# Pooled attention into a routed MoE: x scatters no longer ordered behind x loads of other slots, and loads issued one by one among the scatters

## The chip, the cores and the metric

The kernel runs on one NeuronCore of one Trainium2 chip. The metric is the device time of one execution in microseconds (us); lower is better. Several executions of each kernel are timed in rounds, beside executions of the kernel before on the same chip. One execution of each kernel is also recorded by the hardware profiler. The **span** is the time from the first to the last instruction in that record.

The engines are PE (matmul), DVE (vector), ACT (scalar), POOL (GpSimd) and SP (sync). In this kernel POOL issues nearly all transfers: the loads of q, k, v and of the weights, and every indirect scatter. SP issues the transposing loads of x. All of them run on the core's 16 DMA engines. In the records, q0 is the queue of POOL's transfers (weights and scatters) and q1 the queue of SP's transposes.

A few of the experiments had executions that took 20 to 40 us longer than others of the same kernel. They are called slow, and no conclusion is drawn from a time that only they show.

## The reference, cut to what matters

```python
# attention: B=8, H=8, S=576, D=64; k and v averaged over 8 tokens -> 72 keys
k_p = k.reshape(B, H, 72, 8, D).mean(axis=3)
v_p = v.reshape(B, H, 72, 8, D).mean(axis=3)
attn = softmax(q @ k_p.T / sqrt(D))
x = (attn @ v_p).transpose(0, 2, 1, 3).reshape(4608, 512)
# MoE: each of 4608 tokens has one of 8 experts (domain_id)
for e in range(8):                       # w1[e] 512x1024, w2[e] 1024x512
    out[domain_id == e] = relu(x[domain_id == e] @ w1[e]) @ w2[e]
```

## The kernel before

The kernel has two stages. The attention stage works on four pairs of batches. It writes each chunk of 128 tokens with an indirect scatter into `x_slots` in DRAM, where every expert has 640 slots; slots that no token fills are cleared by other scatters. In the expert stage each expert's x comes back by a transposing load, is multiplied by w1 and w2, and leaves as five blocks of 128 rows, scattered to `out`. Expert 0 is loaded in two parts. Its first 384 slots hold tokens of the first three pairs and can be loaded early. The other 256 slots, called the **late x of expert 0** below, need the last scatters of the attention stage.

```python
def load_pair(t_ap, pr, tag):                     # L84: one of q, k, v of one pair
    t = wp.tile([128, 72, D], F16, tag=tag, bufs=2, name=tag)
    nc.gpsimd.dma_start(...)                      # on POOL
...
def clear(bl):                                    # L370: zeros into empty slots
    i = nc.gpsimd.indirect_dma_start(
        out=x_slots[:], out_offset=bass.IndirectOffsetOnAxis(ap=void[:, bl:bl + 1], axis=0),
        in_=zt[:], ...)                           # L372
    apart(i.ins, "xs", "no token has an empty slot")
    x_scatters.append(i.ins)
...
            if qd == 1:                           # in av_unit: a chunk of 128 tokens is done
                i = nc.gpsimd.indirect_dma_start(
                    out=x_slots[:], out_offset=bass.IndirectOffsetOnAxis(ap=slot_i[:, c:c + 1], axis=0),
                    in_=x_sb[:], ...)             # L508
                apart(i.ins, "xs", "each token has its own slot")
                x_scatters.append(i.ins)
...
def wload(e, which):                              # L532: 1024 KB as float16, from float32
    ...
    nc.gpsimd.dma_start(t, src)                   # L538, on POOL

def xload(e, s0, s1, pool, tag, after=()):        # L543
    xT = pool.tile([128, 4, s1 - s0], F16, tag=tag, bufs=3 if tag == "xT" else 1, name="xT")
    i = nc.sync.dma_start_transpose(xT[:, :, 0:s1 - s0], x_slots[CAP * e + s0:CAP * e + s1, :])   # L545
    behind(i.ins, x_scatters, "x of the slots")   # after all scatters so far
    ...
def l2_units(e, s0, s1, hT):                      # per block of 128 tokens
    ...
    y = late.tile([128, HD], F32, tag="y", bufs=8, name="y")
    ...                                           # PSUM -> y on DVE or ACT
    i = nc.gpsimd.indirect_dma_start(out=out, ..., in_=y[:], ...)    # L590, on POOL
...
tasks = [(0, 0, EARLY), (0, EARLY, CAP)] + [(e, 0, CAP) for e in range(1, E)]

def fetch(e):
    if e >= 2:
        run(clear_units(e))                       # two scatters
    if e == 1:
        xload(0, EARLY, CAP, late, "xTl")         # the late x of expert 0
    wload(e, 0)
    wload(e, 1)
    xload(e, 0, CAP, late, "xT")

fetch(1)
for n, t in enumerate(tasks):
    ...
    u = expert_units(*t)
    nxt = n + 2
    if nxt < E:
        u = u[:3] + [lambda: fetch(nxt)] + u[3:]  # fetch two tasks ahead
    run(u)
```

The dependency tracker sees that a scatter writes `x_slots` and that a transpose reads it. It does not know which rows an indirect scatter touches. So every scatter waits for every transpose that was issued before it, even for a transpose of other experts' slots.

The softmax here doesn't subtract the row's maximum and nothing guards it: scores larger than these inputs give would overflow.

## Time and profile before

| | before |
|---|---|
| timed, median of 2 (range) | 331.55 us (330.36 to 332.73) |
| profiled execution, its time and span | 317.65 and 315.9 us |
| PE busy | 236.0 us, 75% of the span |
| last part of x made by attention (start of the last x_sb, which takes 0.42 us) | 104.9 us |
| PE idle on the two largest releasers in the expert stage | 28.9 + 25.0 us |

Three lines of the page follow: PE's busy time with its share and number of instructions, and the granted PE clock and the DMA busy share in 40 slices of the span, in tenths.

```profile
PE 236.0 (75%) x1888; PEld 161.2 (51%) x1888; DVE 115.9 (37%) x324; ACT 94.4 (30%) x153; POOL 111.3 (35%) x130
...
PEclk9995995989985569759999996559959999879999
DMA  6999999994249532995966959968959949922112
```

The waits view says what each engine waited for (us in total, times, longest). The first fence is PE, the second POOL.

```profile
PE big L565 <- ACT hT L569: 28.9, 4, 19.4
PE big L565 <- DMA xT<-x_slots: 25.0, 3, 13.6
```

```profile
POOL x_slots L372 <- DMA xT<-x_slots: 84.9, 6, 15.8
...
POOL x_slots L508 <- DMA xT<-x_slots: 12.2, 1, 12.2
```

POOL stood still for 84.9 us in six waits of a clear for somebody else's transpose. The timeline shows what lay behind such a wait. Columns are start, duration, engine, line, operation, and in brackets the idle time before it and what ended it. First POOL around the end of attention, then PE in the expert stage.

```profile
100.83 1.01 POOL L508 DMA_INDIRECT x_slots<-x_sb,slot_i  x1 [0.63 <-DVE rcp L500]
114.03 1.00 POOL L508 DMA_INDIRECT x_slots<-x_sb,slot_i  x1 [12.19 <-DMA xT<-x_slots]
...
125.30 1.19 POOL L538 DMA_DIRECT2D w<-in_moe_w_dram  x2
142.28 1.04 POOL L372 DMA_INDIRECT x_slots<-zt,void  x1 [15.80 <-DMA xT<-x_slots]
143.62 1.03 POOL L372 DMA_INDIRECT x_slots<-zt,void  x1 [0.30 <-issue]
144.64 0.60 POOL L538 DMA_DIRECT2D k<-in_moe_w_dram  x1
```

```profile
113.27 7.20 PE L565 MATMUL big<-xT,w 128*128 128x384 f16 x32 [9.68 <-DMA xT<-x_slots]
...
139.23 6.09 PE L565 MATMUL big<-xT,w 128*128 128x256 f16 x32 [13.58 <-DMA xT<-x_slots]
...
206.94 9.13 PE L565 MATMUL big<-xT,q 128*128 128x320 f16 x48 [19.36 <-ACT hT L569]
```

The weights of expert 2 (tiles k and v at 144.64) could only be issued once the clears at 142.28 had been let go. When outputs queue in POOL behind such a wait, the eight y buffers fill, ACT and DVE stop, and PE stops behind them; that is the 19.36 us. The line at 139.23 is the late x of expert 0, for which PE waited 13.58 us.

### The profile page before, as it was taken

Reading aid. Unit: us, or ns where it says so; the run is one execution under the profiler, and the core shown is the slowest. Engines: PE = TensorE matmul, PEld = TensorE weight load, DVE = VectorE, ACT = ScalarE, POOL = GpSimd, SP = SyncE. Lnnn points to the kernel's source line nnn. Section 1 sums busy time; section 2 is a strip of 40 time slices with the busy share of each in tenths; the row PEclk is TensorE's granted clock in tenths of the full one; section 3 lists DMA queues with packets and bytes.
Section 4 is the critical chain, followed back from the end, with each engine's and each line's share of the span. In section 5 each row is a group of like instructions: output and inputs, shape, how many; then the busy total and the mean of one; then the engine's idle time right before and its main releaser. Section 6 shows DMA issues by size and latency. Waiting matters only on the chain.

```text
span 315.9 us, 4766 instructions
## 1 busy us (share of the span) xinstructions
PE 236.0 (75%) x1888; PEld 161.2 (51%) x1888; DVE 115.9 (37%) x324; ACT 94.4 (30%) x153; POOL 111.3 (35%) x130
## 2 busy tenths in 40 slices
PE   0975979879999069039999950079789899399992
PEld 0753655555665044026949530056456685274950
DVE  6630699879688313002323100022112230122410
ACT  1061874567897011002313000022021130121220
POOL 7000161724776048007005036027045066303232
PEclk9995995989985569759999996559959999879999
DMA  6999999994249532995966959968959949922112
GB/s 127 210 221 211 218 216 223 225 213 167 80 92 216 124 98 104 185 196 101 178 178 117 220 107 187 181 123 165 259 115 190 269 66 216 292 84 98 50 68 97
DMA packets 30602, 51.25 MB, mean 162 GB/s; under 512 B 23340, under 2 KB 23406, under 8 KB 26992
## 3 DMA queue, kind: packets, MB, share of 16 engines
q0 software_dynamic: 9728, 45.63, 63.9%
q1 hardware_dynamic: 20848, 5.28, 8.8%
q8 instruction: 15, 0.25, 0.3%
q14 instruction: 11, 0.09, 0.1%
HBM read 61.90 MB, written 17.30 MB: 251 GB/s over the span
## 4 chain that ended last, share of the span: by engine, by line
DMA 47%; PE 21%; issue 13%; DVE 8%; POOL 6%; ACT 2%; POOLq 1%; SPq 0%; ACTq 0%; DVEq 0%
DMA xT<-x_slots 22%; DMA out_dram<-y,orig 9%; DMA k<-in_k_dram 7%; PE big L565 7%; DMA v<-in_moe_w_dram 4%; PE big L474 4%; DMA x_slots<-x_sb,slot_i 3%; POOL out_dram L590 3%; PE small L496 3%; PE small L403 3%; PE small L432 2%; DVE x_sb L503 2%; DMA x_slots<-zt,void 2%; DVE op L326 1%; POOL x_slots L372 1%
## 5 line engine op out<-in xcount | busy, mean ns | idle before, releaser
L565 PE MATMUL big<-xT,w 128*128 128x320 f16 (+2 forms) x256 | 43.2, 333 | 29.6 <-DMA xT<-x_slots 23.3
L571 DVE TENSOR_SCALAR hT<-big 128x640 f16<-128x640 f32 (+2 forms) x36 | 27.0, 749 | 77.2 <-PE big L565 77.2
L565 PEld LDWEIGHTS <-w 128*128 128x128 f16 x256 | 36.3, 149 | 36.7 <-issue 17.8
L590 POOL DMA_INDIRECT out_dram<-y,orig x40 | 39.8, 996 | 39.9 <-DVE y L586 12.4
L508 POOL DMA_INDIRECT x_slots<-x_sb,slot_i x36 | 37.3, 1036 | 45.4 <-DVE rcp L500 16.5
L581 PEld LDWEIGHTS <-hT 128*128 128x128 f16 x320 | 31.4, 98 | 35.9
L477 ACT ACTIVATE at<-big 72x576 f16<-72x576 f32 x64 | 40.5, 645 | 23.8 <-PE big L474 22.9
L569 ACT ACTIVATE hT<-big 128x640 f16<-128x640 f32 (+2 forms) x36 | 23.2, 644 | 79.3 <-PE big L565 79.3
L372 POOL DMA_INDIRECT x_slots<-zt,void x16 | 15.8, 988 | 88.0 <-DMA xT<-x_slots 84.9
L586 DVE COPY y<-small 128x512 f32<-128x512 f32 x20 | 13.8, 692 | 85.8 <-DMA out_dram<-y,orig 51.8
L588 ACT ACTIVATE y<-small 128x512 f32<-128x512 f32 x20 | 12.0, 598 | 94.9 <-DMA out_dram<-y,orig 52.9
L581 PE MATMUL small<-w,hT 128*128 128x512 f16 x160 | 35.3, 379 | 0.0
L503 DVE TENSOR_TENSOR x_sb<-small,rcp 128x256 f16<-128x256 f32 x72 | 30.5, 424 | 2.5
L565 PE MATMUL big<-xT,q 128*128 128x320 f16 x64 | 11.5, 349 | 21.1 <-ACT hT L569 19.4
L496 PE MATMUL small<-vp,at 72*128 72x65 f16 (+1 forms) x320 | 23.9, 215 | 0.7 <-DVE x_sb L503 0.3
L474 PE MATMUL big<-qT,kpT 64*72 64x288 f16 x128 | 22.7, 350 | 1.3 <-ACT qT L462 0.9
L565 PEld LDWEIGHTS <-q 128*128 128x128 f16 x64 | 9.2, 150 | 23.6 <-issue 21.7
L496 PEld LDWEIGHTS <-at 72*128 72x128 f16 (+1 forms) x320 | 16.1, 112 | 9.0 <-issue 4.0
L565 PE MATMUL big<-xT,k 128*128 128x320 f16 x128 | 17.8, 299 | 0.0
L565 PEld LDWEIGHTS <-k 128*128 128x128 f16 x128 | 17.4, 144 | 0.5
L581 PE MATMUL small<-v,hT 128*128 128x512 f16 x80 | 17.6, 379 | 0.0
L403 PE MATMUL small<-k,ident 128*128 128x320 f16 (+1 forms) x64 | 13.2, 349 | 3.6 <-DMA k<-in_k_dram 3.6
(137 smaller groups left out, 221.1 us busy)
## 6 DMA issues: line engine op xcount, KB each, us to landing
w<-in_moe_w_dram POOLq DMA_DIRECT2D x8, 1024.0 KB, 9.0
k<-in_k_dram POOLq DMA_DIRECT2D x4, 1152.0 KB, 22.3
q<-in_q_dram POOLq DMA_DIRECT2D x4, 1152.0 KB, 27.9
v<-in_v_dram POOLq DMA_DIRECT2D x4, 1152.0 KB, 19.8
k<-in_moe_w_dram POOLq DMA_DIRECT2D x3, 1024.0 KB
v<-in_moe_w_dram POOLq DMA_DIRECT2D x3, 1024.0 KB, 13.8
q<-in_moe_w_dram POOLq DMA_DIRECT2D x2, 1024.0 KB
out_dram<-y,orig POOLq DMA_INDIRECT x40, 12.0
```

The lines of the kernel that those rows point to most:

```text
L372: i = nc.gpsimd.indirect_dma_start(out=x_slots[:], out_offset=bass.IndirectOffsetOnAxis(ap=void[:, bl:bl + 1], axis=0), in_=zt[:], in_offs ...
L403: nc.tensor.matmul(pv, ident[:], kk[:, t, w0:w1, :], start=(t == 0), stop=(t == 7))
L474: nc.tensor.matmul(p[0:72, par, 0:288], s["kpT"][64 * par:64 * par + 64, bh, :], s["qT"][64 * par:64 * par + 64, :, 8 * bh:8 * bh + 8], st ...
L477: nc.scalar.activation(at[0:72, bh % 8, :].rearrange("p (a c) -> p a c", a=2), p[0:72, :, 0:288], AFT.Exp, scale=1.0 / 64.0)
L496: nc.tensor.matmul(pv[r0:r0 + z - a, hh, :], s["at", bt][0:72, h, a:z], s["vp"][0:72, 8 * bt + h, :], start=True, stop=True, skip_group_ch ...
L503: nc.vector.tensor_tensor(out=xo, in0=pv[:, :, 0:64].rearrange("p h (a b) -> p b h a", b=4), in1=rcp[:].unsqueeze(1).unsqueeze(3).to_broad ...
L508: i = nc.gpsimd.indirect_dma_start(out=x_slots[:], out_offset=bass.IndirectOffsetOnAxis(ap=slot_i[:, c:c + 1], axis=0), in_=x_sb[:], in_of ...
L565: nc.tensor.matmul(p[:, a, 0:m], w1[:, kk, fi:FF:8], xT[:, kk, m * a:m * a + m], start=(kk == 0), stop=(kk == 3))
L569: nc.scalar.activation(dst, p[:, 0:nh, 0:m], AFT.Relu)
L571: nc.vector.tensor_scalar(out=dst, in0=p[:, 0:nh, 0:m], scalar1=0.0, scalar2=None, op0=ALU.max)
L581: nc.tensor.matmul(p[:], hT[:, fi, 128 * j:128 * j + 128], w2[:, fi, :], start=(fi == 0), stop=(fi == 7))
L590: i = nc.gpsimd.indirect_dma_start(out=out, out_offset=bass.IndirectOffsetOnAxis(ap=orig[:, bl:bl + 1], axis=0), in_=y[:], in_offset=None, ...
```

## The change

The intent: take the false order between scatters and transposes away, so that POOL never waits for a transpose, and spread POOL's loads among the scatters of the attention stage so that no scatter stands behind several loads at once and the weights of experts 0 and 1 are there early.

```diff
@@ clear(), and the same in av_unit() for the scatters of tokens
             apart(i.ins, "xs", "no token has an empty slot")
+            tc.declare_no_dep(i.ins, group="xl", reason="the slots read so far are other experts'")
             x_scatters.append(i.ins)
@@ xload()
-        def xload(e, s0, s1, pool, tag, after=()):
+        def xload(e, s0, s1, pool, tag):
...
+            tc.add_to_no_dep_group("xl", i.ins)
             behind(i.ins, x_scatters, "x of the slots")
-            behind(i.ins, after, "one transfer at a time")
@@ where the plan of the attention stage is made
-        put(clear_units(0) + clear_units(1), 33.0, 40.0)
-        put([lambda: loads(2)], 4.9, 5.0)
-        put([lambda: loads(3)], 15.4, 15.5)
-        put([lambda: wload(0, 0)], 43.0, 43.1)
-        put([lambda: wload(0, 1)], 52.1, 52.2)
-        put([lambda: xload(0, 0, EARLY, per, "xTe")], 52.3, 52.4)
+        for pr in range(2, NP):
+            for d, t_ap, tag, kx in ((kt, k, "k", 6.0), (vt, v, "v", 10.0), (qt_, q, "q", 14.0)):
+                put([lambda d=d, t_ap=t_ap, pr=pr, tag=tag: load(d, t_ap, pr, tag)],
+                    16 * pr - 32 + kx, 16 * pr - 32 + kx)
+        put([lambda: wload(0, 0)], 38.0, 38.0)
+        put([lambda: wload(0, 1)], 43.0, 43.0)
+        put(clear_units(0), 44.0, 46.0)
+        put([lambda: xload(0, 0, EARLY, per, "xTe")], 52.3, 52.3)
+        put(clear_units(1), 60.0, 61.0)
+        put([lambda: wload(1, 0), lambda: wload(1, 1)], 62.0, 63.0)
@@ fetch()
             if e >= 2:
                 run(clear_units(e))
-            if e == 1:
+                wload(e, 0)
+                wload(e, 1)
+            else:
                 xload(0, EARLY, CAP, late, "xTl")
-            wload(e, 0)
-            wload(e, 1)
             xload(e, 0, CAP, late, "xT")
```

(The helper `loads(pr)` for three loads becomes `load(...)` for one.) The change has two parts: the **no-dependence part** (three added lines) and the **placement part** (the rest). A transpose still waits for all scatters issued before it.

More of the change, by code (lines that the diff above doesn't have):

```diff
@@ L511, in av_unit @@
                 apart(i.ins, "xs", "each token has its own slot")
+                tc.declare_no_dep(i.ins, group="xl", reason="the slots read so far are filled by other tokens")
                 x_scatters.append(i.ins)
@@ L617, in put, with load @@
                 plan.append((k0 + (k1 - k0) * (i + 0.5) / len(units), len(plan), f))
-        def loads(pr):
-            kt[pr] = load_pair(k, pr, "k")
-            vt[pr] = load_pair(v, pr, "v")
-            qt_[pr] = load_pair(q, pr, "q")
+        def load(d, t_ap, pr, tag):
+            d[pr] = load_pair(t_ap, pr, tag)
         for pr in range(NP):
```

## The prediction

> **What bounds the kernel now.** PE is 75% busy, DMA 73% (queue list). The attention stage (to 103 us) is nearly PE-bound: PE 14 to 18 us busy in each 17 to 19 us window. The loss is in the expert stage. In the chain of waits the x transposes (xT<-x_slots) are the largest entry, 22% of the span. The waits view says why: POOL's clearing scatters (L372) waited 84.9 us in six times for a transpose of *another* expert to land, and a scatter of L508 12.2 us. POOL works in order, so the next weights and the output scatters stood behind these waits. Outputs came late, the eight y buffers filled, and PE waited: 28.9 us put down to ACT hT (really y and PSUM buffers; DVE and ACT waited 51.8 and 52.9 us for out_dram scatters) and 25.0 us for xT: 54 us idle. Expert DMA comes in saturated bursts (146 to 162 us, 168 to 184, 188 to 210) with gaps.
>
> **What the change does.** No arithmetic is added or removed. In the instruction lists clears and scatters lose only the transpose waits; transposes still wait for scatters. The weights of experts 0 and 1 move forward among the scatters, into a stretch where DMA is under half busy (79 to 98 us: 0.45). The pair loads move later: v2, q2, k3, v3, q3 by about 10 to 20 us. They landed 5 to 20 us ahead of need, so I expect no new stall over 3 us.
>
> **Costed.**
> - Attention ends at about 103 us as before.
> - The first x load landed at 113.3; it should land by 103: the first expert part (12.5 us of PE) starts 8 to 10 us sooner.
> - POOL issues one scatter per 1.29 us and is backlogged from 75 us in both kernels. Without the 12.2 us wait the last scatter goes at about 113 (before 124.3). The late x of expert 0 lands at 120 to 125 instead of 139; PE waits 4 to 9 us instead of 13.6.
> - From there PE needs 10 us for the rest of expert 0 and 17.7 us (8.9 + 8.8) for each of seven more: 134 us, to about 257.
> - DMA, estimated from the bursts: two weights and one x about 14 us, one output scatter about 1.25 us; after 117 us some 140 us of work. So they nearly balance, and I allow 6 us for stalls. Tail after PE 6 us as now.
>
> The Trainium skill, "DMA: Bandwidth & Descriptors", section "Issuing engines are not separate DMA queues", says that all issuers' transfers interleave on the same 16 engines. This trace agrees: a transpose lands in 3.9 us alone, 17.2 us (median) beside weights. So overlap is not free.
>
> Span about 269 us (315.9 before); the timed runs lie 15.7 us above the span, so 284 us, 8 in 10 between 271 and 300. Faster by over 2%: 0.96; same 0.03; slower 0.01.
>
> **What would show it.** L372 waits for xT vanish; PE idle on ACT hT falls from 28.9 to under 8 us; idle on xT from 25 to under 12; DMA share after 113 us rises from about 0.68 to over 0.85; attention end stays within 3 us of 103; last L508 scatter near 113.
>
> **What would make it wrong.** DMA limiting the expert stage (transposes beyond 20 us, outputs queued behind weights, y buffers full again): 295 to 305. Late q3 or v3 stalling attention: some us more. A lower granted clock.

## The result, and the profile after

| | before | after |
|---|---|---|
| timed, median (range), 2 executions each | 331.55 us (330.36 to 332.73) | 301.3 us (300.52 to 302.08) |
| ratio after / before | | 0.9088, 95% interval 0.8916 to 0.926 |
| span of the profiled execution | 315.9 us | 300.4 us |
| start of the last x_sb | 104.9 us | 127.0 us |
| PE resumes with the late x of expert 0 | 139.23 us | 163.05 us |

A ratio in this document is the mean time of one kernel's fast runs over the mean of the other's of the same rounds, so it is not quite the ratio of the medians that are quoted. The change is faster by 9.1%, as predicted in direction, but 301.3 us lies 17 us above the predicted 284 and just outside the range that ended at 300.

The same three lines of the page, after:

```profile
PE 236.1 (79%) x1888; PEld 164.7 (55%) x1888; DVE 117.5 (39%) x324; ACT 95.1 (32%) x153; POOL 110.5 (37%) x130
...
PEclk9995898776987955579555799999999999999998
DMA  6999989897975824698999949999999994302112
```

The waits of PE and of POOL, after:

```profile
PE big L567 <- DMA xT<-x_slots: 23.7, 1, 23.7
```

```profile
POOL out_dram L592 <- ACT y L590: 65.3, 18, 27.3
POOL x_slots L509 <- DVE rcp L501: 44.3, 9, 26.7
```

POOL no longer waits for a transpose at all. The waits it has now are for data to be scattered, which is idle time that costs nothing. PE's 28.9 us on hT are gone too. One wait is left, longer than any before: 23.7 us, once, for a transpose. POOL around the end of attention, then PE:

```profile
130.76 0.98 POOL L509 DMA_INDIRECT x_slots<-x_sb,slot_i  x1 [0.30 <-issue]
...
136.13 0.58 POOL L540 DMA_DIRECT2D k<-in_moe_w_dram  x1 [1.81 <-DMA x_slots<-x_sb,slot_i]
136.69 0.59 POOL L540 DMA_DIRECT2D v<-in_moe_w_dram  x1
...
143.88 0.60 POOL L540 DMA_DIRECT2D q<-in_moe_w_dram  x1
144.47 0.58 POOL L540 DMA_DIRECT2D k<-in_moe_w_dram  x1
```

```profile
125.80 8.34 PE L567 MATMUL big<-xT,w 128*128 128x384 f16 x32
...
163.05 6.62 PE L567 MATMUL big<-xT,w 128*128 128x256 f16 x32 [23.74 <-DMA xT<-x_slots]
...
172.97 8.90 PE L567 MATMUL big<-xT,w 128*128 128x320 f16 x64
...
190.34 8.90 PE L567 MATMUL big<-xT,k 128*128 128x320 f16 x64
```

From 163 us on PE works without a pause, one expert in 17.4 us (190.34 less 172.97), to the end. The late x is read by PE 32 us after the last token scatter at 130.76; before, that was 15 us (139.23 less 124.34). In between POOL has issued the weights of experts 2 and 3, four loads, the first at 136.13 us; before, the first of these loads went at 144.64 us, after the transpose had landed. (The tiles named k, v and q hold weights here: k and v at 136 us are those of expert 2, q and k at 144 us those of expert 3.)

The table by stretch says the same. Columns are the stretch, its length, busy time and instructions of each engine, the mean granted clock, the DMA share and GB/s. First before, then after.

```profile
141.00:170.00 29.00, 29.00 (x175) 21.55 (x174) 7.90 (x12) 7.63 (x13) 10.28 (x12) 0.95 0.66 131
170.00:206.00 36.00, 15.88 (x92) 10.75 (x91) 3.85 (x5) 2.45 (x5) 9.30 (x11) 0.80 0.90 179
206.00:236.00 30.00, 25.85 (x127) 16.93 (x127) 6.83 (x9) 6.09 (x10) 11.03 (x13) 0.79 0.75 163
```

```profile
141.00:170.00 29.00, 6.95 (x35) 5.44 (x36) 1.56 (x4) 1.54 (x4) 3.44 (x5) 0.53 1.05 217
170.00:206.00 36.00, 36.00 (x216) 25.79 (x215) 10.20 (x14) 8.62 (x13) 15.95 (x18) 1.00 0.91 176
206.00:236.00 30.00, 30.00 (x187) 23.09 (x186) 8.88 (x12) 8.03 (x12) 13.64 (x16) 1.00 1.12 229
```

In the stretch from 141 to 170 us PE does 6.95 us of work while the DMA engines are full (1.05). Everywhere later PE is full at a clock of 1.00.

### The profile page after: what moved, and what is told of

It reads as the page before. It is cut to its first block, busy times and chain, and to the rows that moved or that the text cites. A ratio compares the mean times of both kernels' runs of the same rounds, so it can differ in the third digit from the quotient of the medians.

```text
span 300.4 us, 4759 instructions
## 1 busy us (share of the span) xinstructions
PE 236.1 (79%) x1888; PEld 164.7 (55%) x1888; DVE 117.5 (39%) x324; ACT 95.1 (32%) x153; POOL 110.5 (37%) x130
## 4 chain that ended last, share of the span: by engine, by line
issue 33%; DMA 22%; PE 19%; POOL 13%; DVE 6%; ACT 2%; another core or an unknown queue 1%; POOLq 1%
POOL out_dram L592 9%; DMA k<-in_k_dram 7%; DMA out_dram<-y,orig 6%; PE big L475 5%; DMA v<-in_moe_w_dram 4%; PE small L497 4%; DMA w<-in_moe_w_dram 4%; PE small L433 3%; PE small L404 3%; DVE x_sb L504 2%; POOL x_slots L372 1%; PE small L446 1%; PE small L461 1%; DVE qT L465 1%
## 5 line engine op out<-in xcount | busy, mean ns | idle before, releaser
L509 POOL DMA_INDIRECT x_slots<-x_sb,slot_i x36 | 36.4, 1012 | 69.4 <-DVE rcp L501 44.3
L567 PE MATMUL big<-xT,w 128*128 128x320 f16 (+2 forms) x256 | 41.7, 329 | 23.8 <-DMA xT<-x_slots 23.7
L478 ACT ACTIVATE at<-big 72x576 f16<-72x576 f32 x64 | 40.8, 645 | 41.3 <-PE big L475 27.1
L497 PE MATMUL small<-vp,at 72*128 72x65 f16 (+1 forms) x320 | 25.3, 220 | 7.4 <-DVE rcp L501 2.5
L475 PE MATMUL big<-qT,kpT 64*72 64x288 f16 x128 | 24.1, 372 | 4.9 <-issue 1.7
L497 PEld LDWEIGHTS <-at 72*128 72x128 f16 (+1 forms) x320 | 17.0, 115 | 16.9 <-issue 6.1
L433 PE MATMUL small<-ident,v 128*128 128x128 f16 x144 | 17.6, 275 | 7.0 <-DVE kpT L397 5.5
L501 DVE RECIPROCAL rcp<-small 128x4 f32<-128x4 f32 x72 | 12.7, 176 | 17.9 <-PE small L497 10.3
L433 PEld LDWEIGHTS <-v 128*128 128x128 f16 x144 | 12.1, 124 | 10.5 <-issue 7.7
L567 PEld LDWEIGHTS <-k 128*128 128x128 f16 x128 | 17.4, 144 | 0.5
L372 POOL DMA_INDIRECT x_slots<-zt,void x16 | 15.7, 983 | 4.9 <-issue 4.9
```

Source lines behind the costliest of these rows:

```text
L372: i = nc.gpsimd.indirect_dma_start(out=x_slots[:], out_offset=bass.IndirectOffsetOnAxis(ap=void[:, bl:bl + 1], axis=0), in_=zt[:], in_offs ...
L433: nc.tensor.matmul(pv[:, i, :], vv[:, o:o + 128], ident[:], start=(t == 0), stop=(t == 3), skip_group_check=True)
L475: nc.tensor.matmul(p[0:72, par, 0:288], s["kpT"][64 * par:64 * par + 64, bh, :], s["qT"][64 * par:64 * par + 64, :, 8 * bh:8 * bh + 8], st ...
L478: nc.scalar.activation(at[0:72, bh % 8, :].rearrange("p (a c) -> p a c", a=2), p[0:72, :, 0:288], AFT.Exp, scale=1.0 / 64.0)
L497: nc.tensor.matmul(pv[r0:r0 + z - a, hh, :], s["at", bt][0:72, h, a:z], s["vp"][0:72, 8 * bt + h, :], start=True, stop=True, skip_group_ch ...
L509: i = nc.gpsimd.indirect_dma_start(out=x_slots[:], out_offset=bass.IndirectOffsetOnAxis(ap=slot_i[:, c:c + 1], axis=0), in_=x_sb[:], in_of ...
```

## The experiments

Two questions were open. First, the absolute level: attention ended near 127 us in the profile after, but at 104.9 us in the profile before. Either the edit delays attention, or the execution profiled before was a faster one than the timed ones (called the level theory: T2 in the first expectations, P in the last). Second, the late x of expert 0, with two theories. **S**, starvation: the transpose's small packets share the DMA engines with the new weights and only get through when the weights are done. **R**: the last scatters end late, and the transpose has to wait for them. All outputs of all runs were correct. Runs on one chip: e1 to e4; e5 to e8; e9 to e11; e12 to e14.

### Both kernels again, and each part alone

e1_before is the kernel before, unchanged; e2_after the changed kernel, unchanged.

> The kernel before, unchanged, profiled on the same chip as the next three. Theory T1 (the moved loads lengthen the attention stage, from 103 to 125 us): attention ends near 103 us here and the span is near 316 us. Rival T2 (the attention stage varies from chip to chip whatever the placement; the timed runs of before were 331 us against a profiled execution of 317.65): attention ends well after 103 us here, 115 us or more, and the span is near 330 us.

> The changed kernel, unchanged, on the same chip. T1: attention ends near 125 us as in the first profile, over 15 us later than in e1_before. T2: it ends within 5 us of where it ends in e1_before. Both: the second x load of expert 0 takes over 20 us to land, and from there to the end about 137 us.

e3_nodep is the kernel before with only the no-dependence part:

```diff
--- before
@@ clear() and av_unit()
+            tc.declare_no_dep(i.ins, group="xl", reason="...")
@@ xload()
+            tc.add_to_no_dep_group("xl", i.ins)
```

> Only the first part of the change: clears and scatters not ordered behind x loads; loads where they were before. T1: attention ends near 103 us as in before, the late x of expert 0 lands 20 us or more after its issue, because weights of experts 1 to 3 are issued beside it; total 300 us or less, better than or equal to the whole change. If T1 is wrong and the placement is what gains: over 315 us.

e4_place is the changed kernel without those three lines, so only the placement part:

```diff
--- after
@@ clear() and av_unit()
-            tc.declare_no_dep(i.ins, group="xl", reason="...")
@@ xload()
-            tc.add_to_no_dep_group("xl", i.ins)
```

> Only the second part: loads one by one among the scatters; clears and scatters still ordered behind x loads. T1: attention ends near 125 us, no gain or slower than before (325 to 340 us), since the waits of POOL for transposes (85 us) are back. T2: attention as in e1_before, total a few us under before.

| run | this, median us | before, median us | ratio (95%) | start of last x_sb | PE resumes with late x |
|---|---|---|---|---|---|
| e1_before | 332.6 | 331.44 | 1.0071 (0.999 to 1.0153) | 124.3 | 152.46 |
| e2_after | 299.61 | 331.44 | 0.9055 (0.8981 to 0.9128) | 124.4 | 161.21 |
| e3_nodep | 303.14 | 331.44 | 0.9144 (0.9051 to 0.9236) | 128.2 | 164.76 |
| e4_place | 323.6 | 331.44 | 0.9782 (0.9696 to 0.9868) | 121.5 | 146.26 |

The level theory holds. The unchanged kernel's attention ends at 124.3 us here, with a span of 328.2, and the changed kernel's at 124.4. The edit does not delay attention. The profile taken before the prediction was of an execution that took 317.65 us, while the timed ones took 330 to 333.

The no-dependence part alone brings 8.6%, the placement part alone 2.2%, both together 9.5% in the same rounds; the parts nearly add (10.8% against 9.5%). POOL's waits view of e4_place shows that placement leaves the false waits as they were:

```profile
POOL x_slots L372 <- DMA xT<-x_slots: 85.2, 6, 16.2
```

In e2_after and e3_nodep there is no such line, and none of PE waiting for hT either; in e4_place PE still waits 24.9 us for hT. So the mechanism that the change aims at is shown: with the false order of the scatters the wait for hT stands, without it the wait is gone.

From PE's resumption with the late x to the end of the span, e1_before takes 328.2 - 152.46 = 175.7 us and e2_after 298.2 - 161.21 = 137.0 us. The expert stage gains 38.7 us there; 8.8 us of it are given back because the late x is read 8.8 us later.

### What holds the late x of expert 0

e5_hold2 lets the first weights of expert 2 wait for the late x; e6_hold3 does so with those of expert 3 only, so that expert 2's still run beside it. POOL issues in order, so everything after is held too.

```diff
--- after
-        def wload(e, which):
+        def wload(e, which, after=()):
...
-            nc.gpsimd.dma_start(t, src)
+            i = nc.gpsimd.dma_start(t, src)
+            behind(i.ins, after, "weights not beside the x load that is waited for")
...
+        urgent = []
@@ fetch()
-                wload(e, 0)
+                wload(e, 0, urgent if e == 2 else ())     # e6_hold3: e == 3
...
-                xload(0, EARLY, CAP, late, "xTl")
+                urgent.extend(xload(0, EARLY, CAP, late, "xTl"))
```

> The changed kernel, with one wait added: expert 2's first weight load (and all that GpSimd issues after it) waits until the second x load of expert 0 has landed. Theory S (starvation: transposes get few packets while weight packets are queued, so that x load lands only when the queue runs dry, at about 160 us in e2_after, although issued at 135 us): it lands within 5 us of its issue, PE idle on it falls from 24.8 to under 4 us, total 275 to 281 us. Rival R (the x load is late because the last scatters land late, behind the weights of expert 1): at most 3 us gained, 296 to 300 us.

> The same wait one expert later: only expert 3's weights are held; expert 2's (2 loads) are issued beside the x load as in the changed kernel. S: the x load lands when the queue runs dry of two loads less, about 10 us earlier than in e2_after; PE idle on it 12 to 17 us; total 286 to 292 us. R: no gain, 296 to 300 us.

e7_w1early instead brings expert 1's weights forward, before the last nine token scatters; e8_both has this and the edit of e5_hold2.

```diff
--- after
-        put([lambda: wload(1, 0), lambda: wload(1, 1)], 62.0, 63.0)
+        put([lambda: wload(1, 0), lambda: wload(1, 1)], 54.0, 56.0)
```

> The changed kernel with expert 1's weights issued before the last nine scatters instead of before the last five, no hold. R: the last scatters land about 5 us earlier and the x load with them: 5 to 10 us gained, 290 to 295 us. S: the amount queued behind is the same, the x load lands when it is drained: 295 to 300 us; the first x load of expert 0 may be delayed by some us as it now meets these weights.

> Hold of e5 and early weights of e7 together. S: as e5, plus up to 5 us from scatters that land earlier, if the first x load is not delayed past the end of attention: 271 to 280 us.

| run | all its times, us | before, median us | ratio of fast runs (95%) |
|---|---|---|---|
| e5_hold2 | 342.58, 328.03, 319.88, 332.4 | 331.19 | none |
| e6_hold3 | 323.37, 293.13, 311.76, 291.94, 290.68 | 331.19 | 0.8825 (0.872 to 0.893) |
| e7_w1early | 371.76, 345.86, 365.76, 377.14 | 331.19 | none |
| e8_both | 323.26, 295.49, 329.64, 297.26, 293.4 | 331.19 | 0.8941 (0.8831 to 0.905) |

The late x itself is decided before the slow stretches of these profiles begin (about 188 us in e5_hold2, 176 us in e6_hold3), so it can be read from them. PE's timeline, one line each of e2_after, e5_hold2 and e6_hold3:

```profile
161.21 6.01 PE L567 MATMUL big<-xT,w 128*128 128x256 f16 x32 [24.82 <-DMA xT<-x_slots]
```

```profile
141.83 4.43 PE L568 MATMUL big<-xT,w 128*128 128x256 f16 x32 [2.15 <-DMA xT<-x_slots]
```

```profile
154.01 5.77 PE L568 MATMUL big<-xT,w 128*128 128x256 f16 x32 [15.12 <-DMA xT<-x_slots]
```

The wait is 24.8 us with four weight loads let loose beside the transpose (e2_after), 15.12 us with two, and 2.15 us with none. SP issued the late x at 135.45, 137.58 and 138.02 us, so it was no earlier where the wait is short. That is a dose and its response, and it refutes R as the whole cause: with the scatters where they were, the wait all but vanishes. Packet counts from the same records show how. This is a count of the packets that started in each 4 us, worked out from the traces: q1 is the transposes (nearly all of 256 bytes), q0 the KB that weights and scatters moved.

```
us from            132    136    140    144    148    152    156    160    164
before      q1     115   2521    994      0     55     95    262   2180      0
            q0 KB  792    272      0    341    824    752    900     52      0
e2_after    q1       0      6    109    128    345    121    230   3315   3075
            q0 KB  806    688    776    700   1097    832    744      0      0
e5_hold2    q1       0    529   2941    192    115    107    364    113     99
            q0 KB  744    486      0    744    792    636   1137    768    808
e6_hold3    q1       0      0     66     96    458   3403    825    124    115
            q0 KB  868    457    784    744    929     52    496    864    744
```

In every row the transposes move over 2,000 packets per 4 us only where q0 is nearly dry, and 55 to 460 where it is full. (In e2_after the first packet of the late x starts at 139.6 us, so its 6 says nothing.) In e2_after from 140 to 158 us, 756 transpose packets (27 ns each) started beside 758 packets of q0: 374 of 8 KB, which are weights and took 657 ns each, 205 of 4 KB, which are scattered outputs, and small ones. The Trainium skill, "DMA: Bandwidth & Descriptors", section "Queues, rings and completion order", says under Arbitration that each DMA engine goes round between the queues it has work for, a packet at a time. The trace agrees, if a packet of its records is one of the page's: 756 to 758 is one for one; it is 761 to 762 in the first profile after (142 to 160 us) 338 to 338 in e6_hold3 (142 to 151 us), and 115 to 115 in the kernel before (132 to 136 us). An estimate from these numbers: the late x has 1,024 packets (the 5,120 slots take 20,480), 64 for each of the 16 engines; at one per 8 KB packet of 657 ns it would take 42 us. The 758 turns were too few for it, so it landed only when q0 had run dry, at 161.17 us. Theory S holds.

The row of the kernel before shows the irony. There the late x landed at 136 to 140 us, because the next weights stood behind a clear that waited for a transpose. Even there it took 12.2 us (SP issued it at 126.98, it landed at 139.18), beside the weights of expert 1 that POOL had issued at 125.30; in e4_place, where those are loaded earlier, it took 3.8 us (142.46 to 146.21). The false wait that the change removes had also kept the weights out of the way of the one load that PE needed next.

Holding back only the weights of expert 2 doesn't settle it. In e5_hold2 the weights of experts 2 and 3 were issued together after the hold, and from 144 us on the next x met both (the row shows 99 to 364 packets beside a full q0); PE waited 18.4 us for it at 185.72 us. The starvation had moved one expert on. The time expected for e5_hold2, 275 to 281 us, was missed by far; its only fast time, 319.88 us, has no profile, so how much of that the slow transposes took is not known. e6_hold3 came near what was expected (286 to 292 us; fast runs 290.68 to 293.13). e8_both, expected at 271 to 280 us, took 293.4 to 297.26 us in its fast runs, though PE did not wait for the late x in its profile.

Three of e7_w1early's four executions are slow, the profiled one of 371.76 us among them. Before its slow stretch, which begins at about 152 us, it shows two things more. The first x load of expert 0 took 10.1 us on SP instead of 1.5, beside expert 1's weights. And PE did not wait for the late x, without any hold:

```profile
142.13 4.38 PE L567 MATMUL big<-xT,w 128*128 128x256 f16 x32
```

SP issued it at 132.83 us, a microsecond before POOL issued the next weights (133.88), and it landed at 136.69. In e2_after SP issued it at 135.45, after the weights of 134.29. The last token scatter had gone later in e7_w1early (130.34 against 128.15 us), but SP could go 2.5 us after it instead of 7.3, since expert 1's weights, issued at 111.97 us instead of 120.22, no longer stood just before it in q0. So R has a part: late scatters put the transpose behind the new weights, and the weights then starve it. Taking away either one took the wait away. Nothing is concluded from the time of this run.

### All x loads ahead of their weights, and the clears elsewhere

If a transpose beside weights is the trouble, put every x load first. e9_holdall issues x(e) and lets w(e) wait for it, for experts 2 to 7. e10_clears moves all clears into the attention stage, to see whether POOL's clears matter. e11_both does both.

```diff
--- after        (e9_holdall; wload takes after= as in e5_hold2)
@@ fetch()
             if e >= 2:
                 run(clear_units(e))
-                wload(e, 0)
-                wload(e, 1)
             else:
                 xload(0, EARLY, CAP, late, "xTl")
-            xload(e, 0, CAP, late, "xT")
+            x = xload(e, 0, CAP, late, "xT")
+            if e >= 2:
+                wload(e, 0, x)
+                wload(e, 1)
--- after        (e10_clears)
+        put(sum((clear_units(e) for e in range(2, E)), []), 32.5, 46.0)
...
-                run(clear_units(e))
+                pass
```

> The changed kernel, with each expert's x load placed ahead of its weights (experts 2 to 7), the weights waiting for that x load to land. Theory S says x loads starve only beside queued weights, so PE idle on xT falls from 24.8 us to under 8. Theory C (the slow executions of e5 to e8, in which transpose packets took 200 to 700 ns instead of 20 to 40, need new weights that arrive while a transpose runs at full rate) says no execution is slow here: all runs within 2%, 278 to 290 us. If C is wrong: executions over 310 us again.

> The changed kernel with all clearing scatters moved into the attention stage, no hold. x loads of experts 2 and 3 can then be issued without waiting for GpSimd. S: no gain at the x load that PE waits for, which still lands when the weight queue is drained: 294 to 302 us in fast executions; C: slow executions are possible, since the order of weights and x loads is not fixed.

> The holds of e9 with the early clears of e10. S and C: as e9, 276 to 290 us, within 2% of each other; up to 3 us better than e9, since the x load does not wait for the clears.

| run | all its times, us | before, median us | ratio of fast runs (95%) | start of last x_sb |
|---|---|---|---|---|
| e9_holdall | 305.25, 306.45, 299.71, 305.11 | 316.53 | none | 108.6 |
| e10_clears | 324.2, 298.98, 299.88, 299.73, 297.55 | 316.53 | 0.9456 (0.9399 to 0.9514) | 107.2 |
| e11_both | 293.31, 291.99, 292.8, 293.3 | 316.53 | 0.9241 (0.9182 to 0.9299) | 109.2 |

These three ran on a chip on which the kernel before takes 316.53 us and attention ends at 107 to 109 us. So this is the faster level again, the level of the profile that the prediction was made from. Kernels are compared only within the same rounds.

In e9_holdall each of the full x loads takes 2.7 to 3.2 us on SP, where beside weights in e2_after they take 12 to 24 us. Yet what this gains at the late x (PE waits 8.18 us for it) is lost again; 278 to 290 us were expected, and the fastest run took 299.71. PE's waits, then SP's:

```profile
PE big L568 <- ACT hT L572: 30.0, 4, 17.4
PE big L568 <- DMA xT<-x_slots: 9.1, 2, 8.2
```

```profile
SPq L548 <- DMA x_slots<-zt,void: 193.1, 10, 98.4
...
SPq L548 <- PE big L568: 8.8, 4, 3.2
```

The 30.0 us on hT are back, as large as in the kernel before. POOL now waits 12 to 16 us before each expert's first weights, which wait for x(e), and the outputs stand behind the weights in POOL's order. From expert 3 on, x(e) in turn waits for its own two clears (98.4 of SP's 193.1 us lie before the first x load, the rest here), and these stand in q0 behind the weights and outputs issued just before: those of expert 3, the second issued at 142.49 us, had landed at 151.56, and SP started x at 151.58; for expert 4 it was 162.49, 172.52 and 172.66. The same wait that the change took away has been built again with another name. In e11_both, which moves these clears into the attention stage, PE's wait for hT is 9.6 us instead of 30.0. (Its profile shows no slow stretch.)

e10_clears shows PE waiting 27.2 us for the late x with no clear in the way, in a stretch of its profile that is not disturbed. For the late x the clears are not the cause.

### The starved load and the next three x loads as one burst

The last call tried to get both: x without weights beside it, and POOL free afterwards. Three xT buffers and the one of the late x are free when attention ends. e13_burst issues the late x of expert 0 and the x of experts 1, 2 and 3 one after the other, holds only the weights of experts 2 and 3 until the last of these has landed, and leaves the rest as in the changed kernel. Beside it ran the changed kernel again, and e14_both, which is e11_both again on this chip.

```diff
--- after        (e13_burst; wload takes after= as in e5_hold2)
         def fetch(e):
-            if e >= 2:
+            if e == 1:
+                xload(0, EARLY, CAP, late, "xTl")
+            elif e != 3:
                 run(clear_units(e))
-                wload(e, 0)
+            if e == 2:
+                run(clear_units(3))
+            x = ()
+            if e < 3:
+                x = xload(e, 0, CAP, late, "xT")
+            if e == 2:
+                x = xload(3, 0, CAP, late, "xT")
+            if e >= 2:
+                wload(e, 0, x)
                 wload(e, 1)
-            else:
-                xload(0, EARLY, CAP, late, "xTl")
-            xload(e, 0, CAP, late, "xT")
+            if e > 3:
+                xload(e, 0, CAP, late, "xT")
```

> The changed kernel again, on whatever chip this call gets. Theory P (the 20 us by which attention ends earlier in the profile that the prediction was made from belong to the chip, not to the kernel): where before measures near 316 us here, attention ends near 105 us and the total is 280 to 298 us; where before measures near 331 us, attention ends near 124 us and the total is 297 to 302 us. Against P: attention near 105 us beside a before of 331 us, or the reverse.

> The x loads of experts 0 (second part), 1, 2 and 3 go alone, ahead of the weights of experts 2 and 3, which wait for them; everything later as in the changed kernel. Theory S: PE idle on the second x load of expert 0 falls from some 24 us to under 5, and in executions without the slow transposes the total is 15 to 22 us under e12_after. If S gives the gain back: y buffers or weights of expert 2 late, PE idle over 10 us on something else, total within 6 us of e12_after.

> The kernel of e11 again, beside e12_after on one chip. If e11's version beats the changed kernel: 3 to 10 us under e12_after, with no slow execution in four. If e11's 293 us was only the faster chip: the same as e12_after or slower.

| run | all its times, us | before, median us | ratio (95%) | start of last x_sb | PE resumes with late x |
|---|---|---|---|---|---|
| e12_after | 300.75, 302.08, 303.92, 302.2 | 332.08 | 0.91 (0.902 to 0.918) | 125.6 | 162.15 |
| e13_burst | 288.18, 290.5, 289.29, 290.04 | 332.08 | 0.8716 (0.8642 to 0.8789) | 127.0 | 141.45 |
| e14_both | 304.67, 305.46, 304.32, 307.21 | 332.08 | 0.9188 (0.9103 to 0.9273) | 139.8 | 154.70 |

e13_burst beats both kernels. Its mean is 289.50 us against 302.24 us of the changed kernel in the same rounds, a ratio of 0.958, and the times of the two do not overlap. A gain of 15 to 22 us was expected; it is 12.7. Its packets in each 4 us, counted as above, show the burst:

```
us from            132    136    140    144    148    152    156    160    164
e13_burst   q1       0   1002   2732   3038   2060      0      0      0      0
            q0 KB  900    158      0      0      0    592    832    772   1172
```

PE's timeline of e13_burst around the late x, and the largest wait after it:

```profile
141.45 5.62 PE L568 MATMUL big<-xT,w 128*128 128x256 f16 x32 [3.37 <-DMA xT<-x_slots]
...
190.82 9.67 PE L568 MATMUL big<-xT,q 128*128 128x320 f16 x48 [3.37 <-ACT hT L572]
```

The wait for the late x is 3.37 us instead of 24.6, so PE resumes 20.7 us sooner than in e12_after. From there to the end it takes 286.4 - 141.45 = 144.95 us instead of 299.0 - 162.15 = 136.85 us: 8.1 us are given back, among them the 3.37 us at 190.82. The profiles' spans differ by 12.6 us.

e14_both shows why runs must be read by stage. On the earlier chip the same kernel took 291.6 us of span, here 303.0. From its resumption with the late x (142.38 and 154.70 us) to the end it took 149.2 and 148.3 us, which is the same. The whole difference lies before that point.

### The slow state, left open

In some executions of e5_hold2, e6_hold3, e7_w1early, e8_both and e10_clears, the transposes themselves became slow. Their packets took some 200 to 820 ns on average over many 4 us stretches instead of the usual 16 to 55, and q0 fell from about 800 to mostly between 50 and 440 KB per 4 us, although work was queued. PE then waited up to 58 us (e7_w1early). It was seen in no profile or time of the two kernels, nor in e3_nodep, e4_place, e9_holdall, e11_both, e13_burst or e14_both. Theory C was that it begins when new weights arrive while a transpose is running at its full rate. The runs without it agree with C where x and weights never overlap (e9_holdall, in part e11_both), but the later x loads of e13_burst do overlap with weights and were not slow. So C is not shown, and the cause stays open.

## Why the prediction was right or wrong

**Right: the bottleneck and what the change does to it.** The waits of L372 for xT vanished (84.9 us to none). PE's idle time on hT fell from 28.9 us to none, where under 8 was predicted. In e4_place, without the no-dependence part, both stayed. The first expert part starts with no wait for its x (before 9.68 us). The tail and the pace of 17.4 us per expert were right too.

**Wrong, first step: "The late x of expert 0 lands at 120 to 125 instead of 139; PE waits 4 to 9 us instead of 13.6."** The wait measured 23.7 us, and 24.8 and 24.6 in the two repeats. The prediction costed the late x from the last scatter and took a few us for the load, although it said itself that a transpose takes 3.9 us alone and 17.2 beside weights. It did not ask what POOL would issue next once nothing held it: four weight loads, right into that transpose. The prediction named contention as what could go wrong ("DMA limiting the expert stage: 295 to 305"), and the time did fall there, but the form was another. DMA did not limit the stage: PE never paused after 163 us. One load was starved, once. (Two of the nine transposes, the late x and the one behind it, did go "beyond 20 us", as that passage had named: 25.7 and 27.1 us from SP to landing.)

**Wrong, second step: "Attention ends at about 103 us as before" together with "the timed runs lie 15.7 us above the span".** The difference of 15.7 us is not an overhead of timing. The profiled execution itself took 317.65 us, 1.7 us above its span, and that stood in the same record as the span. It was an execution at a faster level than the timed ones. On the chips where the kernel before takes 331 to 332 us, attention ends at 121 to 128 us in both kernels (except e14_both, with its clears moved); where it takes 316.5 us, at 107 to 109. "As before" was right on the same chip (124.3 and 124.4); the 103 us was not.

**The sum.** Counting from where the first expert part could begin to the end of the span, 269 - 103 = 166 us were predicted and 300.4 - 125.80 = 174.6 measured, 8.6 us more: +17.2 for the late x (23.7 against the middle of 4 to 9), +1.0 for the first part, and -9.6 for the rest, where the 6 us allowed for stalls were not needed. For the level, attention came 22.8 us later than predicted (125.80 against 103), and the offset of the timed run was 1.7 us instead of 15.7, which takes 14.0 us back: +8.8. Together 17.4 us, the distance from 284.7 (269 + 15.7) to the 302.08 us of the profiled execution. Two errors of level partly cancelled. With the right offset alone the prediction would have been worse.

**The gain, seen from the other side.** The same stretch of the kernel before is 328.2 - 123.0 = 205.2 us in e1_before, where the first part could have begun at 123.0 (126.39 less its wait of 3.38). In the profile that the prediction was made from it was 315.9 - 103.6 = 212.3 us, of which the longer first wait (9.68 against 3.38) is 6.3. So about 7 us of the loss that I meant to remove did not exist in the timed executions.

**Checks that failed as a result.** Idle on xT was to fall under 12 us and was 23.7. The last token scatter was to go near 113 us and went at 130.76, with attention. The DMA share after 113 us was to exceed 0.85 and was about 0.76, the mean over six stretches to the end; it is 0.91 to 1.12 from 141 to 236 us, but the transfers are done early, and the last 64 us are quiet (0.52 and 0.22). The statement of the Trainium skill, "DMA: Bandwidth & Descriptors", section "Issuing engines are not separate DMA queues", that all issuers' transfers interleave on the same engines, was right and was the warning: SP's transpose was starved by POOL's loads.

**The clock adds a little to this wait.** The Trainium skill, "TensorE: Matmul & The Clock Gate", Part 1, says that PE's clock has two states, half and full, and falls to half after idling. The records of both kernels have only 0.5 and 1.0. After the 23.7 us of waiting in the changed kernel the clock stays at 0.5 until 169.1 us, 6.0 us after PE resumed; the page gives about 3.4 us of sustained work, counted in a window that runs freely, and 6.0 us (4.3 in e2_after) lies between one such window and two. The same 32 matmuls took 6.62 us there and 4.43 us after the short wait of e5_hold2, so the cold clock costs about 2.2 us on top.

## What to carry to other kernels

A wait that looks false may still do work: before it is removed, ask what the engine behind it will issue next, and which transfer in flight that will meet. Here a load of small packets beside queued loads of large packets did not get half of the DMA engines' time, it got one packet for each packet of theirs, and landed when they were done. So issue such a load ahead of the large ones, or hold these until it has landed, and do this once where it matters: holding back POOL for every expert brought the old stall back (30.0 us on hT in e9_holdall). Before a span and a time are joined in one sum, check that they are of the same execution or at the same level.

## What the Trainium skill lacked or had wrong

- "DMA: Bandwidth & Descriptors", "Queues, rings and completion order", states the arbitration but not what follows for a load of small packets. Here one 256 byte packet of the transposes went for each packet of the other queue (756 to 758 in 18 us), most of them of 4 or 8 KB, so the turns were equal in packets and not in bytes: the transposes fell from over 3,000 packets per 4 us alone to 55 to 460 beside weights, and an x load of 2.7 to 3.2 us took 12 to 24 us.
- No page describes the slow transposes: packets of some 200 to 820 ns instead of 16 to 55, with the weights' rate down to 50 to 440 KB per 4 us.
- No page says that the same single-core kernel can run at different levels on different chips: 316.53 us on one and 331 to 332 us on three others, with attention ending at 107 to 109 or at 121 to 128 us. The cause is open.
